# Making a projected weight in four double bursts instead of eight, with its input tiles in lent buffers

## The chip, the core and the metric

The kernel runs on one core of a Trainium2 chip. The core has five engines with an instruction order of their own: TensorE (PE: matmuls; PEld: its weight loads), VectorE (DVE), ScalarE (ACT), GpSimd (POOL) and SyncE (SP, which here only issues transfers). They meet through semaphores: an instruction whose input or whose output place isn't free holds up everything behind it in its engine's order. Matmuls add up in PSUM, which has eight banks (b0 to b7); everything else lies in SBUF. The metric is the device time of one execution in microseconds, median of several runs.

## The reference, cut to what matters

Two branches over the same x (2048 tokens, 640 wide), mixed by a gate:

```python
a = einsum("bsd,ed->bse", x, dft_hid_re); b = einsum("bsd,ed->bse", x, dft_hid_im)
y = einsum("ts,bse->bte", dft_seq_re, a) - einsum("ts,bse->bte", dft_seq_im, b)      # branch A

q = einsum("nd,dhc->nhc", xf, w_q)                     # 32 heads, 256 wide
s1 = einsum("nhd,ed->nhe", q[..., :dk], k1); s2 = einsum("nhd,ed->nhe", q[..., dk:], k2)
# top 2 of each, top 2 of their 4 sums, softmax -> g, expert numbers top_e       # branch B
act = gelu(einsum("nd,nhkd->nhk", xf, u[top_e]))
out = einsum("nhk,nhk,nhkd->nd", g, act, v[top_e])

gate = sigmoid((x * gate_w).sum(-1)); result = gate * y + (1 - gate) * out
```

All values are float32. The kernel never forms q: it multiplies w_q by the keys k1 and k2 first, which gives one matrix W' of 640 x 1024 (64 half-heads by 16 keys), and then scores x against W'.

## The kernel before, in words

Each float32 matmul is made of three passes in a reduced format: an operand is split into a rounded half h (ScalarE, line 138) and a remainder l (VectorE or POOL, line 139), and `mm3` (lines 143 to 145) adds h*h, h*l and l*h into a bank.

The first half of the kernel walks over *pieces* (`seq_piece`, line 229). A piece is 128 rows of a sequence matrix by 512 columns: `pieces = [(w, c, s) ...]`, s running fastest over the 16 row tiles, c over 4 column blocks, w over the real and the imaginary matrix. Piece n multiplies x tile s = n % 16 by it into banks 0 to 4, 15 matmuls of 512 columns. Pieces 0 to 15 are the first column block, 16 to 31 the second; behind pieces 15 and 31 ScalarE empties the five banks (line 252), and piece 16 or 32 then begins them anew. While TensorE is at piece n, the program issues the load of piece n + 5 (five buffers, `wf`) and the split of piece n + 3 (a ring of four, `WS`).

Everything else is hung between the pieces by `at(n, f, ...)`: the function f is emitted behind piece n (`follow(n)`), and calls for one n are emitted in the order in which they were registered. Instructions of each engine run in the order in which they were emitted; nobody reorders them. In the first `N0` = 30 pieces these are hung in:

- `load_x` (line 284), `split_x` (290), `gate_sum` (315): behind piece n the load of x tile n + 4, the split of tile n + 3 (ScalarE, VectorE), and the gate's sum of tile n + 2 (VectorE, line 318). Raw x lies in three buffers of two tiles each, with the tags xf, xh, xl.
- `load_wq` and `w_part` (388, 393): w_q comes in 32 tiles of 640 KB, four to each of 8 groups G, into five buffers. A *burst* is the four tiles of a group: 16 float32 matmuls of 320 columns (32 records, line 400), into two banks drawn in turn from 5 and 6 (`ps_s`). When a bank is complete, VectorE transposes it into wp[G] (line 406).
- `split_w` (408) splits wp[G] into W', kept in `WH` and `WL`. `make_t` (415), for groups 4 to 7, makes four sums of W's blocks with six VectorE instructions (lines 428 to 433) and splits them (ScalarE and VectorE, four times) into `TW`, which lies where x tiles 0 to 5 were.
- `put_x` and `get_x` (484, 487): x tiles 0 to 10 are stored to DRAM after use and fetched again; `move_x` copies tiles 11 and 12 aside.
- `load_u`, `split_u` (439, 443): the expert table u, five tiles, split into `UH` and `UL`; `load_xT`, `split_xT` (POOL), `sum_xT` (VectorE, lines 472 to 475): the first pair of transposed x tiles.

Behind piece 31 the scoring begins (`score_step`, 583), four steps to a pair of x tiles, each behind a piece of its own. Its first step uses W' of groups 0 to 3 and bank 5, splits the sums of x (ScalarE, then POOL) and copies a bank (line 587); its second step needs that copy and `TW`.

In the kernel before, group G's burst is hung behind piece 6 + 3G, so at 6, 9, 12 ... 27:

```python
    for G in range(NG):
        b = 6 + 3 * G
        for m in range(4 * G, 4 * G + 4):
            at(b, w_part, m)
        at(b, split_w, G)
        if G >= NG // 2:
            at(b + (4, 3, 2, 1)[G - NG // 2], make_t, G)
```

These lines are registered behind those of x, so behind one piece `load_x`, `split_x` and `gate_sum` come first.

Of the kernel before, what the change touches and what calls it, by code (L numbers as in the profile page):

```python
# [8 lines left out]
F32 = mybir.dt.float32  # L9
F32R = mybir.dt.float32r  # L10
# [7 lines left out]
P = 128  # L18
S = 2048
D = 640  # L20
H = 32
E = 16
HH = 2 * H
WARM = 11
NE = E * E
NT = S // P
NP = NT // 2
TC = 512
NC = S // TC
NPC = 2 * NC * NT  # L30
KD = D // P
HALF = D // 2
NG = HH // 8
# [73 lines left out]
def gated_mix_kernel(ctx: ExitStack, tc: tile.TileContext, xT, xn, dreT, dimT, wsre, wsim, wq, kT, uT, vv, gw, out):  # L107
    nc = tc.nc
# [3 lines left out]
    big = ctx.enter_context(tc.tile_pool(name="big", bufs=1))  # L112
# [5 lines left out]
    def rotate(what, n):  # L118
        turn[what] = (turn.get(what, -1) + 1) % n
        return turn[what]  # L120

    def bank(n, shape=(P, TC), dt=F32):
        return psum.tile(list(shape), dt, name=f"b{n}", tag=f"b{n}")

    def ps_s(shape=(P, TC)):
        return bank(5 + rotate("pss", 2), shape)

    def ps_t(shape, dt=F32):
        return bank(7, shape, dt)

# [5 lines left out]
    def split(f, h, l, eng):  # L136

        nc.scalar.activation(h, f, AF.Copy)  # L138
        eng.tensor_sub(l, f, h.bitcast(F32))  # L139

    def mm3(o, wh, wl, ah, al, first, last, more=False):

        nc.tensor.matmul(o, wh, ah, start=first, stop=False, skip_group_check=more)  # L143
        nc.tensor.matmul(o, wh, al, start=False, stop=False, skip_group_check=more)  # L144
        nc.tensor.matmul(o, wl, ah, start=False, stop=last, skip_group_check=more)  # L145
# [9 lines left out]
    def run_bg(us):  # L155
        bg.run(us, share)


    WU = big.tile([P, 2 * KD * (HH * E + NE)], F32R, name="WU", tag="WU")
    NW = KD * HH * E  # L160
    WH, WL = (WU[:, n * NW:(n + 1) * NW].rearrange("p (k c) -> p k c", k=KD) for n in range(2))
    UH, UL = (WU[:, 2 * NW + n * KD * NE:2 * NW + (n + 1) * KD * NE].rearrange("p (k c) -> p k c", k=KD)
              for n in range(2))
    zc = const.tile([P, NT], F32)
    gt, gc = (const.tile([P, 2 * NT], F32, name=t) for t in ("gt", "gc"))

# [2 lines left out]
    N0 = 3 * NG + 6  # L169
# [26 lines left out]
    def at(n, f, *args):  # L196
        then.setdefault(n, []).append(lambda: f(*args))
# [57 lines left out]
    for q in range(2 * NC):  # L255
        n = NT * (q + 1)
# [83 lines left out]
    t = ps_t([P, TC])  # L340
    for n in range(WARM):
        c = slice(0, 2 * P) if n < WARM - 1 else slice(2 * P, TC)
# [41 lines left out]
    wqs, wps, wp = {}, {}, {}  # L384
    WQB = 5
    NWQ = 4 * NG

    def load_wq(m):
        if m < NWQ:
            wqs[m] = p1.tile([P, 4, HALF], F32, name="wq", bufs=WQB)  # L390
            nc.sync.dma_start(wqs[m], wq[m])

    def w_part(m):
        G, r, n = m // 4, m // 2 % 2, m % 2
        if r == 0:
            wps[G, n] = ps_s()
        ps = wps[G, n]
        w = wqs.pop(m)
        for j in range(4):
            nc.tensor.matmul(ps[32 * j:32 * j + 32, :HALF], kp[:, 8 * G // H, r, :], w[:, j], start=(r == 0),  # L400
                             stop=(r == 1))
        if r == 1:
            if n == 0:
                wp[G] = p1.tile([P, KD, P], F32, name="wp", bufs=2)
            t = wp[G].rearrange("p k (j c) -> p j k c", c=32)[:, 2 * n:2 * n + 2]
            nc.vector.transpose(t, wps.pop((G, n))[:, :HALF].rearrange("p (j k c) -> p j k c", j=2, c=32))  # L406
# [27 lines left out]
        for n in range(1, 5):  # L434
            split(t[:, n - 1], *(w[:, :, c] for w in TW[n]), nc.vector)

    uf = {}

    def load_u(k):
        uf[k] = p1.tile([P, NE], F32, name="uf", tag="uf", bufs=2)  # L440
        nc.sync.dma_start(uf[k], uT[k])

    def split_u(k):
        split(uf.pop(k), UH[:, k], UL[:, k], nc.vector)


    xf, xs = {}, {}
# [41 lines left out]
        nc.sync.dma_start(X[s].bitcast(F32), xd[s])  # L489

    for s in range(9):
        at(6 + 2 * s + (3 if s == 8 else 0), put_x, s)
    for s in range(3):
        at(2 * NT - 5 + s, get_x, s, 6 + s)
    for s, tag in ((11, "xh"), (12, "xl")):
        at(s + 5, move_x, s, tag)
    for n in range(NT - 4):
        at(n, load_x, n + 4)
    for n in range(NT - 3):
        at(n, split_x, n + 3)  # L500
    for n in range(NT - 2):
        at(n, gate_sum, n + 2)
    for m in range(WQB):
        at(m, load_wq, m)

    for G in range(NG):
        b = 6 + 3 * G
        for m in range(4 * G, 4 * G + 4):
            at(b, w_part, m)
        at(b, split_w, G)  # L510
        if G >= NG // 2:
            at(b + (4, 3, 2, 1)[G - NG // 2], make_t, G)
        for i, m in enumerate(range(4 * G + WQB, 4 * G + WQB + 4)):
            at(b + (i // 2 if G < 4 else 0), load_wq, m)
    for s in range(9, AWAY):
        at(b - 1, put_x, s)
    n = b + 2
    at(n - 8, load_xT, 0)
    for k in range(KD):
        at(n - 15 + 2 * k, load_u, k)  # L520
        at(n - 13 + 2 * k, split_u, k)
    for a in range(2):
        at(n - 2, split_xT, 0, a)
    at(n - 1, sum_xT, 0)
# [58 lines left out]
    def score_step(p, a):  # L583
# [4 lines left out]
        if a == 0:  # L588
# [3 lines left out]
            if p % 2:  # L592
                u_pairs(p // 2)
# [170 lines left out]
    def put_act(c, n):  # L764

        if n == 0:
            f = p2.tile([P, TC], F32, name="act")
        elif c < NC - 1:
            f = ROWS[1].rearrange("p a b c -> p (a b c)").bitcast(F32)[:, :TC]
        else:  # L770
            f = big.tile([P, TC], F32, name="act", tag="xf")
        nc.scalar.activation(f, AB.pop(("u", n)), AF.Gelu_apprx_tanh)
        AB["act", n] = f
# [5 lines left out]
    def u_pairs(c):  # L779


        xh, xl = xs["xh"], xs["xl"]

        for n in range(2):
            e = slice(n * P, (n + 1) * P)
            AB["u", n] = ps = bank(7 - n)
            for k in range(KD):
                mm3(ps, UH[:, k, e], UL[:, k, e], xh[:, :, :, k, :], xl[:, :, :, k, :], k == 0, k == KD - 1)
                run_bg(0.68)
            if n == 0:  # L790
                put_act(c, 0)

    for p in range(NP):
        n = N0 + 4 * p + min((p + 1) // 2, 3)
# [3 lines left out]
    for n in range(2 * NT + 3, 4 * NT + 3):  # L798
        s = n % NT
# [104 lines left out]
        while masked or unmasked:  # L904
            yield settle(True)

    DD = VH = VL = None
    draw = {}

    def load_dd(m):  # L910

# [4 lines left out]
                nc.sync.dma_start(draw[m][:, a], (dreT, dimT)[w][k])  # L916

    def split_dd(m, a):
        nonlocal DD
        if DD is None:  # L920
            DD = big.tile([P, 2, 2, KD, D], F32R, name="DD", tag="WU")
        w, k = divmod(2 * m + a, KD)
        split(draw[m][:, a], DD[:, w, 0, k], DD[:, w, 1, k], nc.gpsimd)
        if a == 1:
            draw.pop(m)

# [2 lines left out]
    for m in range(KD):  # L929
        for a in range(2):  # L930
            at(N1 + 6 + 5 * m + 2 * a, split_dd, m, a)
        at(N1 + 11 + 5 * m, load_dd, m + 2)
# [11 lines left out]
    TS, T = {}, {}  # L944
# [6 lines left out]
    def t_sum(k, n, a):  # L951

        m = 8 if k == KD else k
        if n < 2:
            return TS[m][:, (2 * n + a) * 2 * P:][:, :2 * P]
        if n == 2:
            return TS[5 + k // 2][:, (2 * (k % 2) + a) * 2 * P:][:, :2 * P]
        return right(0, a, k)[:, 2 * P:4 * P] if n == 3 else TS[m][:, PAIR + a * P:][:, :P]

    def right(w, a, k):  # L960
        return T[("xh", "xl")[a]][:, w] if k == KD else DD[:, w, a, k]

    def make_sums(k):
        if k in (0, KD):
# [104 lines left out]
    for k, (n, m) in enumerate(((-1, 2), (0, 4), (5, 7), (7, 9), (10, 12))):  # L1069
        n, m = NT * (NC + 2) + n, NT * (NC + 2) + m  # L1070
# [89 lines left out]
    def step(m):  # L1160
        b, (u, k) = m // NSTEP, divmod(m % NSTEP, KZ)
        what = UNITS[u]
        if k == 0:
# [8 lines left out]
        split_step(m + AHEAD)  # L1172
        o, w, w5 = {
            "a11": ("X", lambda a: right(0, a, k)[:, 0:2 * P], lambda a: right(0, a, k)[:, 4 * P:]),
            "a12": ("Z", lambda a: right(1, a, k)[:, 0:2 * P], lambda a: right(1, a, k)[:, 4 * P:]),
            "s1": ("Y", lambda a: t_sum(k, 0, a), lambda a: right(0, a, k)[:, 4 * P:]),
            "s2": ("X", lambda a: t_sum(k, 1, a), None),
# [146 lines left out]
```

## Time and profile before

| | |
|---|---|
| median of 3 runs (lowest to highest) | 749.91 us (749.51 to 750.06) |
| the profiled execution | 749.66 us |
| its span, first to last instruction | 747.8 us |
| TensorE busy | 743.5 us, 99% |
| VectorE, ScalarE, POOL busy | 589.9, 364.2, 342.9 us |
| moved by DMA | 171.11 MB, mean 229 GB/s |

The profile is of one execution. Busy is the union of the instructions' durations; TensorE's matmuls overlap in it, so a TensorE that is 99% busy may still lose time between two starts, which is why starts are compared. "L400" is line 400 of the kernel before. In a row of a timeline stand the start, the duration, the engine and line, the operation, the tile written and the tiles read, the count of records, and in brackets the idle time ahead of it with what ended it. In the chain of waits stand start, duration and what held the end up. In the windows stand the stretch and its length, each engine's busy time (with its count of instructions), TensorE's granted clock, the share of the DMA engines and GB/s.

### The profile page before, as it was taken

What the parts mean: (1) busy time and instruction counts of PE and PEld (TensorE: products, weight loads), DVE (VectorE), ACT (ScalarE), POOL (GpSimd) and SP (SyncE); (2) the same over time, 40 slices, a digit from 0 to 9 for tenths busy, and PEclk for the clock granted to TensorE, in tenths of its full rate; (3) what the DMA queues carried; (4) which work ended last, traced back from release to release, by engine and by line L of the source; (5) the groups of instructions that cost most, each with busy time, mean ns of one, the idle gap of its engine ahead of it and who ended that gap; (6) DMA issues with size and microseconds to landing.
All of it is one profiled execution on the core that took longest, in us unless ns stands there. A gap on an engine that the chain in (4) does not pass through costs nothing.

```text
span 747.8 us, 11144 instructions
## 1 busy us (share of the span) xinstructions
PE 743.5 (99%) x3923; PEld 603.7 (81%) x3923; DVE 589.9 (79%) x744; ACT 364.2 (49%) x664; POOL 342.9 (46%) x287
## 2 busy tenths in 40 slices
PE   9999999999999999999999999999999999999998
PEld 7767777888888888888888888888888888888887
DVE  7865378395999899999999888979999974357651
ACT  4335144543544745555463686633545653443351
POOL 5533225440532424145235456643455793487253
PEclk9999999999999999999999999999999999999999
DMA  9999999787566686972498776479865689775301
GB/s 335 397 384 343 379 357 391 203 218 240 138 173 149 188 240 163 230 200 73 116 400 281 159 167 188 140 239 292 287 214 196 225 263 344 216 236 176 112 29 71
DMA packets 84633, 171.11 MB, mean 229 GB/s; under 512 B 16097, under 2 KB 21601, under 8 KB 84321
## 3 DMA queue, kind: packets, MB, share of 16 engines
q1 hardware_dynamic: 70960, 146.13, 57.5%
q0 software_dynamic: 5472, 9.96, 9.0%
q10 hardware_dynamic: 8144, 14.31, 5.1%
q8 instruction: 31, 0.51, 0.3%
q14 instruction: 26, 0.20, 0.1%
HBM read 136.40 MB, written 32.39 MB: 226 GB/s over the span
## 4 chain that ended last, share of the span: by engine, by line
PE 92%; DMA 6%; DVE 1%; ACT 0%; SPq 0%; issue 0%
PE b L143 30%; PE b L144 30%; PE b L145 30%; DMA xr<-in_xn 3%; DMA wq<-in_wq 3%; PE b L400 2%; PE b L877 1%; DVE xr L318 0%; DVE X L139 0%; ACT X L138 0%; DVE wp L406 0%; SPq L322 0%; SPq L288 0%; ACT WU L138 0%; DVE WU L139 0%
## 5 line engine op out<-in xcount | busy, mean ns | idle before, releaser
L143 PE MATMUL b<-WS,X 128*128 128x512 f32 x620 | 243.3, 392 | 0.0
L144 PE MATMUL b<-WS,X 128*128 128x512 f32 x620 | 241.4, 389 | 0.0
L145 PE MATMUL b<-WS,X 128*128 128x512 f32 x620 | 241.3, 389 | 0.0
L139 POOL TENSOR_TENSOR WS<-wf,WS 128x512 fp32r<-128x512 f32 x89 | 132.8, 1497 | 166.7 <-ACT WS L138 157.5
L143 PEld LDWEIGHTS b<-WS,X 128*128 128x128 f32 x620 | 116.4, 188 | 28.3 <-issue 3.1
L145 PEld LDWEIGHTS b<-WS,X 128*128 128x128 f32 x620 | 116.4, 188 | 24.3
L144 PEld LDWEIGHTS b<-WS,X 128*128 128x128 f32 x620 | 116.4, 188 | 23.5
L138 ACT ACTIVATE WS<-wf 128x512 fp32r<-128x512 f32 x89 | 55.2, 625 | 70.8 <-PE b L145 30.3
L865 DVE TENSOR_TENSOR hot<-rows,wtab 128x1024 f16<-128x1024 f16 x64 | 60.6, 973 | 2.6 <-PE b L877 2.6
L139 POOL TENSOR_TENSOR xl<-xf,xh 128x640 fp32r<-128x640 f32 x16 | 27.0, 1691 | 71.6 <-ACT xh L138 71.6
L587 ACT ACTIVATE sc<-b 128x512 f32<-128x512 f32 x32 | 19.8, 620 | 80.8 <-PE b L145 77.0
L191 POOL DMA_DIRECT2D WS<-in_wsre x30 | 26.4, 879 | 62.3 <-ACT WS L189 60.9
L139 POOL TENSOR_TENSOR WS<-ra,WS 128x512 fp32r<-128x512 f32 x33 | 47.1, 1437 | 14.6 <-ACT WS L138 12.6
L138 ACT ACTIVATE WS<-ra 128x512 fp32r<-128x512 f32 x47 | 29.4, 631 | 42.5 <-PE b L145 28.2
L835 ACT ACTIVATE b<-b,mask 128x128 f32<-128x128 f32 x128 | 43.0, 342 | 13.4 <-PE b L877 10.3
L642 DVE TENSOR_TENSOR eq<-sc,mm 128x1024 f16<-128x1024 f32 x32 | 44.4, 1388 | 0.9
L649 DVE TENSOR_REDUCE tied<-eq 128x64 f32<-128x1024 f16 x32 | 39.0, 1219 | 0.9
L640 DVE TENSOR_REDUCE mm<-sc 128x64 f32<-128x1024 f32 x32 | 38.8, 1211 | 0.2
L139 POOL TENSOR_TENSOR WP<-ra,WP 128x512 fp32r<-128x512 f32 x13 | 19.2, 1491 | 31.0 <-ACT WP L138 30.9
L217 DVE SCALAR_TENSOR_TENSOR ST<-ST,grow 128x512 f32<-128x512 f32 x40 | 31.3, 846 | 1.1 <-DMA grow<-gdr 1.1
L143 PE MATMUL b<-WU,xh 128*128 128x512 f32 x80 | 31.1, 389 | 0.0
L144 PE MATMUL b<-WU,xh 128*128 128x512 f32 x80 | 31.1, 389 | 0.0
(216 smaller groups left out, 1449.8 us busy)
## 6 DMA issues: line engine op xcount, KB each, us to landing
X<-xd SPq DMA_DIRECT2D x36, 640.0 KB, 6.6
wq<-in_wq SPq DMA_DIRECT2D x32, 640.0 KB, 8.2
wf<-in_wsim SPq DMA_DIRECT2D x64, 256.0 KB, 4.8
wf<-in_wsre SPq DMA_DIRECT2D x63, 256.0 KB, 6.7
ra<-pd SPq DMA_DIRECT2D x40, 256.0 KB, 3.2
pd<-ST ACTq DMA_DIRECT2D x35, 256.0 KB, 5.3
WS<-in_wsre POOLq DMA_DIRECT2D x30, 256.0 KB, 6.3
xd<-X SPq DMA_DIRECT2D x11, 640.0 KB, 9.5
```

The costliest lines, as they stand in the source:

```text
L138: nc.scalar.activation(h, f, AF.Copy)
L139: eng.tensor_sub(l, f, h.bitcast(F32))
L143: nc.tensor.matmul(o, wh, ah, start=first, stop=False, skip_group_check=more)
L144: nc.tensor.matmul(o, wh, al, start=False, stop=False, skip_group_check=more)
L145: nc.tensor.matmul(o, wl, ah, start=False, stop=last, skip_group_check=more)
L191: nc.gpsimd.dma_start(l, (wsre, wsim)[w][c, s], accum_op=OP.add)
L217: nc.vector.scalar_tensor_tensor(f, f, -1.0 if w else 1.0, g, op0=OP.mult, op1=OP.mult)
L640: nc.vector.tensor_reduce(m, sc, op=OP.max, axis=AX.X)
L642: nc.vector.tensor_tensor(eq, sc, m[:, :, None].to_broadcast([P, HH, E]), op=OP.is_equal)
L649: nc.vector.tensor_reduce(tied[:, s, ib, :], eq, op=OP.add, axis=AX.X)
L835: nc.scalar.activation(f[:, :, n], f[:, :, n], AF.Copy, scale=mask4[:, n:n + 1])
L865: nc.vector.tensor_tensor(o, a, b, op=op)
```

## The change

- The eight bursts become four of two groups each, behind pieces 10, 16, 22 and 28. The groups of a burst use the same two banks: bank 5 + n, with n the half of the group.
- Within a group the two tiles that add into one bank now come one after the other (tile numbers are permuted when loaded).
- The w_q tiles are loaded on other pieces: 0 to 8 behind pieces 0 to 8, then two or so ahead of each burst. Beside the five buffers they lie in places idle at the time: the places of x tiles 14, 15 and 6 to 8, raw x buffers, and a new tile `wqu`, where u's split table goes later. u's table therefore leaves `WU`, and one slice of a later table (`DD`) lies in its place.
- u is loaded and split on pieces 22 to 28 instead of 14 to 24; the moves of x tiles 11 and 12 go from pieces 16 and 17 to 23 and 24; the store of x tile 8, three fetches of x and the load of x transposed shift by one to three pieces.
- `make_t` of groups 4 to 7 goes from pieces 22, 24, 26, 28 to 23, 24, 28, 29.

```diff
-    def ps_s(shape=(P, TC)):
-        return bank(5 + rotate("pss", 2), shape)
...
+    WU = big.tile([P, 2 * NW], F32R, name="WU", tag="WU")
+    wqu = big.tile([P, 2, 4, HALF], F32, name="wqu", tag="UU")
...
+    BURST = 8
+    LENT_WQ = {5: "X15", 6: "X14", 15: "xl", 16: "xf", 17: "xh", 23: "xl", 29: "X6", 30: "X7", 31: "X8"}
+    LENT_U = {7: 1, 8: 0, 14: 1, 18: 0}
...
-        if m < NWQ:
+        if m in LENT_U:
+            wqs[m] = wqu[:, LENT_U[m]]
+        elif m in LENT_WQ:
+            wqs[m] = big.tile([P, 4, HALF], F32, name="wq", tag=LENT_WQ[m])
+        else:
             wqs[m] = p1.tile([P, 4, HALF], F32, name="wq", bufs=WQB)
-            nc.sync.dma_start(wqs[m], wq[m])
+        nc.sync.dma_start(wqs[m], wq[m // 4 * 4 + m % 2 * 2 + m // 2 % 2])
...
-        G, r, n = m // 4, m // 2 % 2, m % 2
+        G, n, r = m // 4, m // 2 % 2, m % 2
         if r == 0:
-            wps[G, n] = ps_s()
+            wps[G, n] = bank(5 + n)
...
-        at(6 + 2 * s + (3 if s == 8 else 0), put_x, s)
-    for s in range(3):
-        at(2 * NT - 5 + s, get_x, s, 6 + s)
+        at(6 + 2 * s, put_x, s)
     for s, tag in ((11, "xh"), (12, "xl")):
-        at(s + 5, move_x, s, tag)
+        at(s + 12, move_x, s, tag)
...
+    n = N0 - 1
+    for B in range(NWQ // BURST):
+        b = 10 + 6 * B
+        for m in range(BURST * B, BURST * (B + 1)):
             at(b, w_part, m)
+        for a in range(2):
+            G = 2 * B + a
+            at(b + (a if b < n - 1 else 0), split_w, G)
+            if G >= NG // 2:
+                at(min(b + 1, n - 1) + a, make_t, G)
+    for b, m in enumerate((0, 1, 2, 3, 4, 5, 6, 7, 8)):
+        at(b, load_wq, m)
+    for m, b in enumerate((10, 10, 11, 11, 12, 12, 13, 14, 16, 16, 16, 17, 18, 19, 20, 20, 22, 22, 22, 22, 23, 24, 25), 9):
+        at(b, load_wq, m)
     for s in range(9, AWAY):
+        at(n - 3, put_x, s)
+    for s, b in enumerate((28, 28, 29)):
+        at(b, get_x, s, 6 + s)
+    at(n - 7, load_xT, 0)
     for k in range(KD):
-        at(n - 15 + 2 * k, load_u, k)
-        at(n - 13 + 2 * k, split_u, k)
+        at(n - 7 + k, load_u, k)
+        at(n - 5 + k, split_u, k)
```

More of the change, by code (lines that the diff above doesn't have):

```diff
@@ L156, in run_bg @@
         bg.run(us, share)
-    WU = big.tile([P, 2 * KD * (HH * E + NE)], F32R, name="WU", tag="WU")
     NW = KD * HH * E
+    WU = big.tile([P, 2 * NW], F32R, name="WU", tag="WU")
+    wqu = big.tile([P, 2, 4, HALF], F32, name="wqu", tag="UU")
     WH, WL = (WU[:, n * NW:(n + 1) * NW].rearrange("p (k c) -> p k c", k=KD) for n in range(2))
-    UH, UL = (WU[:, 2 * NW + n * KD * NE:2 * NW + (n + 1) * KD * NE].rearrange("p (k c) -> p k c", k=KD)
-              for n in range(2))
     zc = const.tile([P, NT], F32)
@@ L435, in make_t @@
             split(t[:, n - 1], *(w[:, :, c] for w in TW[n]), nc.vector)
-    uf = {}
+    uf, UHL = {}, []
     def load_u(k):
@@ L443, in split_u @@
     def split_u(k):
-        split(uf.pop(k), UH[:, k], UL[:, k], nc.vector)
+        if not UHL:
+            t = big.tile([P, 2, KD, NE], F32R, name="UU", tag="UU")
+            UHL.extend(t[:, n] for n in range(2))
+        split(uf.pop(k), *(t[:, k] for t in UHL), nc.vector)
     xf, xs = {}, {}
@@ L502, in gated_mix_kernel @@
         at(n, gate_sum, n + 2)
[L503 to L508, printed above, removed]
-            at(b, w_part, m)
[L510 to L514, printed above, removed]
+    n = N0 - 1
+    for B in range(NWQ // BURST):
+        b = 10 + 6 * B
+        for m in range(BURST * B, BURST * (B + 1)):
+            at(b, w_part, m)
+        for a in range(2):
[7 more added lines that the diff above has]
+        at(b, load_wq, m)
     for s in range(9, AWAY):
-        at(b - 1, put_x, s)
-    n = b + 2
-    at(n - 8, load_xT, 0)
+        at(n - 3, put_x, s)
+    for s, b in enumerate((28, 28, 29)):
+        at(b, get_x, s, 6 + s)
+    at(n - 7, load_xT, 0)
     for k in range(KD):
-        at(n - 15 + 2 * k, load_u, k)
-        at(n - 13 + 2 * k, split_u, k)
+        at(n - 7 + k, load_u, k)
+        at(n - 5 + k, split_u, k)
     for a in range(2):
@@ L787, in u_pairs @@
             for k in range(KD):
-                mm3(ps, UH[:, k, e], UL[:, k, e], xh[:, :, :, k, :], xl[:, :, :, k, :], k == 0, k == KD - 1)
+                mm3(ps, UHL[0][:, k, e], UHL[1][:, k, e], xh[:, :, :, k, :], xl[:, :, :, k, :], k == 0, k == KD - 1)
                 run_bg(0.68)
@@ L905, in experts @@
             yield settle(True)
-    DD = VH = VL = None
-    draw = {}
+    DD, draw = [], {}
     def load_dd(m):
@@ L918, in split_dd @@
     def split_dd(m, a):
-        nonlocal DD
-        if DD is None:
-            DD = big.tile([P, 2, 2, KD, D], F32R, name="DD", tag="WU")
+        if not DD:
+            t = big.tile([P, 2, 2, KD - 1, D], F32R, name="DD", tag="WU")
+            DD.extend(t[:, :, :, k] for k in range(KD - 1))
+            DD.append(big.tile([P, 2, 2, D], F32R, name="DD", tag="UU"))
         w, k = divmod(2 * m + a, KD)
-        split(draw[m][:, a], DD[:, w, 0, k], DD[:, w, 1, k], nc.gpsimd)
+        split(draw[m][:, a], DD[k][:, w, 0], DD[k][:, w, 1], nc.gpsimd)
         if a == 1:
@@ L960, in right @@
     def right(w, a, k):
-        return T[("xh", "xl")[a]][:, w] if k == KD else DD[:, w, a, k]
+        return T[("xh", "xl")[a]][:, w] if k == KD else DD[k][:, w, a]
     def make_sums(k):
```

## The prediction

> **What bounds the kernel now.** I read the page first, then TensorE's timeline, the chain of waits, the windows, and last the other engines around the two places that the change touches. From the page:
>
> ```profile
> span 747.8 us, 11144 instructions
> PE 743.5 (99%) x3923; PEld 603.7 (81%) x3923; DVE 589.9 (79%) x744; ACT 364.2 (49%) x664; POOL 342.9 (46%) x287
> ```
>
> TensorE is the bound, and almost nothing is left between its instructions. So a microsecond in which it waits is a microsecond lost, and whatever shortens its own stream is gained. TensorE's timeline of the stretch that the change rewrites:
>
> ```profile
> 17.95 0.39 PE L143 MATMUL b<-WS,X 128*128 128x512 f32 x1
> ...
> 27.92 0.39 PE L145 MATMUL b<-WS,X 128*128 128x512 f32 x1
> 28.24 2.36 PE L400 MATMUL b<-wq,kp 128*32 128x320 f32 x32
> 30.53 0.50 PE L143 MATMUL b<-WS,X 128*128 128x512 f32 x1
> 30.87 0.40 PE L144 MATMUL b<-WS,X 128*128 128x512 f32 x1
> ...
> 53.67 1.82 PE L400 MATMUL b<-wq,kp 128*32 128x320 f32 x24
> 55.76 0.75 PE L400 MATMUL b<-wq,kp 128*32 128x320 f32 x8 [0.27 <-DMA wq<-in_wq]
> ```
>
> The first row is the first matmul of piece 4; pieces 4 to 6 are 45 matmuls and end where the first burst begins, so a piece is (28.24 - 17.95 - 0.09)/3 = 3.40 us, or 0.227 us per matmul. Starts, not durations, are to be read: durations overlap. From 27.92 to 30.87 lie 2.95 us; two matmul slots off (0.45) leave 2.50 us as the whole price of a one-group burst. Eight records of a burst take 2.36 - 1.82 = 0.54 us, so 32 take 2.16; the other 0.34 us is the price of entering and leaving a burst. The third burst was cut by a late w_q tile: it ended at 55.76 + 0.75 = 56.51 and not at 53.67 + 2.36 = 56.03, a loss of 0.48 us.
>
> TensorE is full, but in the first 65 us the transfers are full too. The windows (last two columns: share of the DMA engines, GB/s) and the chain of waits:
>
> ```profile
> 5.00:25.00 20.00, 20.00 (x92) 16.59 (x91) 17.29 (x23) 8.61 (x14) 13.60 (x11) 1.00 1.03 397
> 25.00:45.00 20.00, 20.00 (x132) 14.12 (x131) 14.72 (x20) 5.87 (x10) 8.20 (x23) 1.00 1.02 386
> ```
>
> ```profile
> 20.92 9.12 DMA xr<-in_xn
> ...
> 30.07 0.74 ACT X L138
> ...
> 30.84 0.83 DVE X L139
> 31.67 0.73 DVE xr L318
> ...
> 32.41 0.84 DVE wp L406 x2
> ...
> 34.70 10.56 DMA xr<-in_xn
> ```
>
> The chain shows an x tile landing at 30.04 (x9), ScalarE rounding it, VectorE taking the remainder and the gate's sum, and only then VectorE transposing the burst's result, though TensorE had finished that burst at 30.5. The transposes stand behind the x tile in VectorE's order. Today this costs nothing: the next burst, which needs the banks, comes three pieces later.
>
> **The change, part by part.**
>
> *Fewer entries.* Eight bursts become four: 4 x 0.34 = 1.35 us less on TensorE (at least 0.8, if only the 0.09 before and 0.11 behind a burst are saved). The matmuls are the same; their order inside a group changes which of two banks comes when, and I price that at nothing, since successive matmuls of a piece already accumulate into one bank at 0.227. The 0.48 us of the third burst should go too: the new loads for a burst are issued pieces ahead.
>
> *A new wait in the first burst.* Both groups of a burst use banks 5 and 6. Group 1's first matmul must wait until VectorE has transposed group 0's first bank, with the whole of TensorE's order behind it. In VectorE's order of piece 10 stand, ahead of that transpose, the remainder of x13 and the gate's sum of x12. When does x13 land? It is issued at piece 9, in both kernels behind the same transfers: from x9 on, four w_q tiles (5 to 8), four pieces, two stores of x and x10 to x13.
>
> ```profile
> 36.93 0.33 SPq L288 DMA_DIRECT2D xr<-in_xn  x1
> ```
>
> ```profile
> xr<-in_xn SPq DMA_DIRECT2D x1, 320.0 KB, 9.8
> ```
>
> ```profile
> wq<-in_wq SPq DMA_DIRECT2D x32, 640.0 KB, 8.2
> ...
> wf<-in_wsre SPq DMA_DIRECT2D x63, 256.0 KB, 6.7
> ...
> xd<-X SPq DMA_DIRECT2D x11, 640.0 KB, 9.5
> ```
>
> Measured, x13 lands at 36.93 + 9.8 = 46.7. By bytes: 4 x 640 + 4 x 256 + 2 x 640 + 4 x 320 = 6144 KB, 6.29 MB, at 386 to 400 GB/s 15.7 to 16.3 us behind 30.04: 45.8 to 46.3. It cannot come earlier because SP waits less: the DMA share is already over 1. I take 46.2. Then 0.75 (ScalarE) + 0.83 + 0.82 (VectorE, rows of the chain) + 0.42 (half of the two transposes) = 49.0. TensorE, with no burst at pieces 6 and 9, ends piece 10 at 17.95 + 7 x 3.40 = 41.75 and group 0 at 41.75 + 0.09 + 2.16 = 44.0. It stands **5.0 us**. Bounds: 4.4 with the landing at 45.8; 6.8 with 46.7 and VectorE's instructions at their slow price, which they have while POOL works:
>
> ```profile
> 51.84 1.91 DVE L318 CUSTOM_DVE_ANT_0 xr<-xr,gwb 128x640 f32<-128x640 f32 x1
> ```
>
> The bursts behind 16 and 22 have no x tile ahead of their transposes; a bank is free about 0.6 us after its matmuls and asked for 1.1 us after them. No stall there.
>
> *The last burst moves from piece 27 to 28 and holds two groups.* Let E be the first matmul behind it. Now and here:
>
> ```profile
> 117.71 2.36 PE L400 MATMUL b<-wq,kp 128*32 128x320 f32 x32
> 120.00 0.50 PE L143 MATMUL b<-WS,X 128*128 128x512 f32 x1
> ...
> 135.09 0.39 PE L143 MATMUL b<-WS,X 128*128 128x512 f32 x1
> ```
>
> ```profile
> 119.60 1.06 DVE L406 STREAM_TRANSPOSE wp<-b 128x320 f32<-128x320 f32 x2 [1.43 <-PE b L400]
> 121.25 0.56 DVE L139 TENSOR_TENSOR WU<-wp,WU 128x384 fp32r<-128x384 f32 x1 [0.59 <-ACT WU L138]
> 121.72 0.42 DVE L428 TENSOR_TENSOR tt<-wp,WU 128x256 f32<-128x256 f32 x1
> ...
> 128.84 0.42 DVE L139 TENSOR_TENSOR WU<-tt,WU 128x256 fp32r<-128x256 f32 x1
> 129.18 1.52 DVE L472 TENSOR_TENSOR xf<-xf 128x256 f32<-128x256 f32 x1
> ```
>
> ```profile
> 131.25 0.63 ACT L189 ACTIVATE WS<-WS 128x512 fp32r<-128x512 f32 x1
> 131.78 2.75 ACT L252 ACTIVATE ST<-b 128x512 f32<-128x512 f32 x5
> ...
> 135.66 0.58 ACT L587 ACTIVATE b<-b 128x512 f32<-128x512 f32 x1
> ```
>
> Piece 32 needs the banks that ScalarE empties behind piece 31, and asks for the first at 135.09, E + 15.1 today. Behind piece 28 one piece less lies between: E + 11.7. ScalarE reaches that emptying only through its order: halves of both groups' W', of group 6's sums, of u's last tile, piece 32, halves of group 7's sums, pieces 33 and 34. The sums of a group (ten VectorE instructions) took 128.84 + 0.42 - 121.72 = 7.5 us beside POOL, and 3.85 without it, by these rows (nine in 3.47):
>
> ```profile
> 98.37 0.41 DVE L429 TENSOR_TENSOR tt<-wp 128x256 f32<-128x256 f32 x1
> ...
> 101.42 0.42 DVE L139 TENSOR_TENSOR WU<-tt,WU 128x256 fp32r<-128x256 f32 x1
> ```
>
> ```profile
> 121.92 3.36 POOL L139 TENSOR_TENSOR xl<-xf,xh 128x640 fp32r<-128x640 f32 x2 [2.61 <-ACT xh L138]
> ```
>
> In the new order that POOL work (x transposed, piece 27) is done before the burst, and POOL waits for ScalarE, so I take the fast price. From E: W' of both groups ready 1.8 (121.81 - 120.00 today), group 6's sums 5.65, u 6.0, the sums of x 8.8 (four instructions: 1.7 all fast, 3.9 with two at the 1.52 of L472, taken 2.8 with one), group 7's last half on ScalarE 8.8 + 2.4 + 0.5 = 11.7, pieces 33 and 34 three times 0.6, 13.5, the first emptying 14.1. Piece 32 starts 2.4 late. ScalarE goes on: four more emptyings 2.2, four halves of x's sums 1.4, the copy of the bank (L587) 0.55, at 18.3; TensorE is through piece 32 at 14.1 + 3.4 = 17.5 and waits 0.8 more. Together **3.2 us**; bounds 0, if ScalarE gets through its list 3 us faster than summed, and 7, if one group's sums keep their slow price.
>
> *At nothing.* The w_q tiles in lent places: the raw x buffers and u's table are idle then; the latest, in X8, can be issued when piece 24 is through, 13.6 us before the burst behind 28, against 10.6 us, the longest landing quoted; without that cover the burst would wait up to the difference. u's tiles come two pieces before they are split, 6.8 us, and have landed in up to 10.6; SP runs about three pieces ahead of TensorE, which covers it; if not, VectorE is late for the last burst by about 3 us, and that goes into the upper bound. The two moved copies of x on ScalarE fall at pieces 23 and 24 with no one waiting. The table's new place is read as before.
>
> *The sum.* Against the profiled execution's own 749.66: 749.66 - 1.35 - 0.48 + 5.0 + 3.2 = 756.0. That execution is 0.25 under the median, so **756.3**.
>
> **The rivals.** *The first stall alone* (VectorE and ScalarE keep up after piece 28): 753.1. For it: today's list ends well ahead of 135.09; against it: it gets twice the work and one piece less.
>
> *No stall; the bursts only merge.* 749.91 - 1.35 - 0.48 = 748.1, faster. The mechanism is the landing of x13: from 49.0 back to 44.0, it would have to land by 41.2, that is 5 us before the bytes allow it. Against it is the DMA share of 1.02; for it, only that the lent places let SP issue w_q tiles 5 to 8 earlier. The second stall would have to vanish too.
>
> *Both stalls, and a slow clock behind the first.* At the start TensorE ran 256 columns in 0.23 us, half the pace of later:
>
> ```profile
> 0.77 2.51 PE L343 MATMUL b<-const-bfloat16-1.0 128*128 128x256 bf16 x11 [0.77 <-PEq L1316]
> ```
>
> If a wait of 5 us puts it back into that state for as long as this row lasts, 2.51 us pass at half pace and 1.25 are lost: 757.6. The trace has no wait of that length to show it. [...]
>
> *More than summed* (slow sums in the last burst, or a late u tile): 749.91 - 1.83 + 5.0 + 7 = 760.1, and 763.1 with 6.8 in the first burst and the clock.
>
> **How the numbers follow.** Both stalls 0.47 (its own range 754 to 759), with the slow clock 0.12, first stall alone 0.16, more than summed 0.09, no stall 0.16. The range leaves out the last and the top of the one before: 752 to 762.5. Some 0.2%, 1.5 us, is what a measurement here tells from no change. No stall lies at the edge of it: 0.10 faster, 0.06 same; with 0.02 from a smaller first stall, same is 0.08, slower 0.82.
>
> **What would show it.** Right: a gap on TensorE inside the first burst, between the 32nd and the 33rd record, ended by VectorE's L406; a gap before piece 32 ended by ScalarE's L252; four bursts of 64 records at about 4.6 us where nothing waits. Wrong: a first burst of 64 records without a gap (then x13 was there, and the queue of transfers is not what I read), piece 32 on time, or a burst waiting for a w_q tile.

## The result and the profile after

The changed kernel takes 755.43 us (median), the kernel before 749.91: a ratio of 1.0077, 95% interval 1.0051 to 1.0102. It is slower, by some 5 us. Its undisturbed runs fall in three places: 754.31, 754.50 and 754.75 at a granted TensorE clock of 1.00, 756.11 at 0.998, and 759.20 at 0.993; a sixth run, at 825.99 us with a clock of 0.851, was disturbed and counts in the median but not in the ratio, and so does one of 930.95 us (0.753) in the first experiment. The profiled execution is the one of 754.75 us. In the changed kernel the lines are renumbered: L405 is the burst's matmul (was L400), L411 the transpose (was L406), L140 to L142 are `mm3`, L135 and L136 the two halves of a split, L314 is the gate's sum, L248 the emptying of the banks (was L252).

The head of the page after:

```profile
span 753.0 us, 11145 instructions
PE 743.4 (99%) x3923; PEld 604.8 (80%) x3923; DVE 577.6 (77%) x744; ACT 366.1 (49%) x664; POOL 341.7 (45%) x287
```

The span grew by 5.2 us, TensorE's busy time not at all. So TensorE waits longer, and the page alone doesn't say where. TensorE's timeline of the kernel after does:

```profile
18.76 0.39 PE L140 MATMUL b<-WS,X 128*128 128x512 f32 x1
...
42.65 2.36 PE L405 MATMUL b<-wq,kp 128*32 128x320 f32 x32
48.05 1.82 PE L405 MATMUL b<-wq,kp 128*32 128x320 f32 x24 [3.03 <-DVE wp L411]
...
120.78 0.39 PE L142 MATMUL b<-WS,X 128*128 128x512 f32 x1
121.09 4.51 PE L405 MATMUL b<-wq,kp 128*32 128x320 f32 x64
125.54 0.50 PE L140 MATMUL b<-WS,X 128*128 128x512 f32 x1
125.88 0.40 PE L141 MATMUL b<-WS,X 128*128 128x512 f32 x1
...
137.00 0.39 PE L142 MATMUL b<-WU,xl 128*128 128x512 f32 x1
139.85 0.50 PE L140 MATMUL b<-WS,X 128*128 128x512 f32 x1 [2.46 <-ACT ST L248]
```

Inside the first burst, group 0's 32 records are issued by 42.65 + 2.16 = 44.81, and the next record starts at 48.05: 3.24 us lost, ended by VectorE's transpose. The last burst, whose banks come free in time, runs through: from the matmul ahead of it to the second one behind it lie 5.10 us, 4.65 without two matmul slots, against 2 x 2.50 for two single bursts, so 0.35 us is saved. Piece 32 starts 2.85 us behind the matmul ahead of it and not 0.23: 2.62 us lost, ended by ScalarE's emptying. The chain of waits of the kernel after tells what lies behind both:

```profile
36.77 8.43 DMA xr<-in_xn
45.23 0.75 ACT X L135
45.99 0.83 DVE X L136
46.82 0.73 DVE xr L314
47.56 0.44 DVE wp L411
48.05 2.36 PE b L405 x32
...
136.74 0.44 DVE tt L438
137.52 0.61 ACT WS L135
138.13 0.53 ACT WS L184
139.22 0.59 ACT ST L248
139.85 0.50 PE b L140
```

First x13's landing, its two halves, the gate's sum of x12, and only then the transpose for which TensorE waits; later VectorE's last sum of group 7, then ScalarE's pieces 33 and 34, and only then the emptying of piece 31's banks.

The landing ends the first wait, but it is only just the last thing waited for. VectorE's timeline has the gate's sum of x11 right ahead, and VectorE then stands idle for 0.40 us until x13's first half is there:

```profile
43.69 1.90 DVE L314 CUSTOM_DVE_ANT_0 xr<-xr,gwb 128x640 f32<-128x640 f32 x1
...
45.99 0.83 DVE L136 TENSOR_TENSOR X<-xr,X 128x640 fp32r<-128x640 f32 x1 [0.40 <-ACT X L135]
```

So an earlier x13 alone would have taken at most 0.40 us off the wait; the rest is what else stands ahead of the transpose in VectorE's order.

The terms add up: 749.66 (profiled execution before) - 4 x 0.35 - 0.48 + 0.81 (piece 4 begins at 18.76, not at 17.95) + 3.24 + 2.62 + 0.34 (three gaps of 0.11 to 0.12 behind the start of piece 32: two restarts and the copied bank) = 754.79; the profiled execution after took 754.75.

### The profile page after: what moved, and what is told of

The parts are those of the page before. It is cut to its first block, busy times and chain, and to the rows that moved or that the text cites. A ratio compares the mean times of both kernels' runs of the same rounds, so it can differ in the third digit from the quotient of the medians.

```text
span 753.0 us, 11145 instructions
## 1 busy us (share of the span) xinstructions
PE 743.4 (99%) x3923; PEld 604.8 (80%) x3923; DVE 577.6 (77%) x744; ACT 366.1 (49%) x664; POOL 341.7 (45%) x287
## 4 chain that ended last, share of the span: by engine, by line
PE 91%; DMA 4%; DVE 3%; issue 1%; ACT 0%; SPq 0%; ACTq 0%
PE b L140 30%; PE b L142 29%; PE b L141 29%; PE b L405 2%; DMA xr<-in_xn 2%; DMA wq<-in_wq 1%; PE b L888 1%; DMA wf<-in_wsre 1%; DVE xr L314 1%; DVE X L136 0%; DVE WU L136 0%; ACT X L135 0%; DVE xf L481 0%; DVE wp L411 0%; DVE tw L136 0%
## 5 line engine op out<-in xcount | busy, mean ns | idle before, releaser
L140 PE MATMUL b<-WS,X 128*128 128x512 f32 x620 | 243.0, 392 | 2.5 <-ACT ST L248 2.5
L142 PE MATMUL b<-WS,X 128*128 128x512 f32 x620 | 241.3, 389 | 0.0
L136 POOL TENSOR_TENSOR WS<-wf,WS 128x512 fp32r<-128x512 f32 x89 | 133.2, 1499 | 173.0 <-ACT WS L135 171.8
L140 PEld LDWEIGHTS b<-WS,X 128*128 128x128 f32 x620 | 116.4, 188 | 29.0 <-ACT ST L248 2.9
L142 PEld LDWEIGHTS b<-WS,X 128*128 128x128 f32 x620 | 116.4, 188 | 24.3
L135 ACT ACTIVATE WS<-wf 128x512 fp32r<-128x512 f32 x89 | 55.7, 626 | 84.1 <-PE b L142 55.6
L876 DVE TENSOR_TENSOR hot<-rows,wtab 128x1024 f16<-128x1024 f16 x64 | 57.9, 931 | 4.4 <-PE b L888 4.4
L136 POOL TENSOR_TENSOR xl<-xf,xh 128x640 fp32r<-128x640 f32 x16 | 26.8, 1675 | 73.5 <-ACT xh L135 67.1
L136 POOL TENSOR_TENSOR WS<-ra,WS 128x512 fp32r<-128x512 f32 x33 | 46.7, 1424 | 14.4 <-ACT WS L135 12.4
L135 ACT ACTIVATE WS<-ra 128x512 fp32r<-128x512 f32 x47 | 29.4, 631 | 42.4 <-PE b L142 28.2
L136 POOL TENSOR_TENSOR WP<-ra,WP 128x512 fp32r<-128x512 f32 x13 | 19.0, 1471 | 31.2 <-ACT WP L135 31.2
L876 DVE TENSOR_TENSOR hot<-hot,rows 128x1024 f16<-128x1024 f16 x32 | 31.5, 985 | 0.0
L140 PE MATMUL b<-WU,xh 128*128 128x512 f32 x80 | 31.2, 391 | 0.0
```

The source lines that it names most:

```text
L876: nc.vector.tensor_tensor(o, a, b, op=op)
```

## The experiments

The theory: two waits, independent of each other, make up the whole loss; the first is as long as x13's landing is late, the second as long as the list ahead of ScalarE's emptying. The rivals: the waits only show a loss that has its cause elsewhere (the transfers, a slower clock), so that taking one away gives nothing back; or the slow clock behind a wait is a large part of it. Each experiment is an edit of the changed kernel, compared with the kernel before on the same chip (749.67 to 749.82 us).

**The first burst cut in two: its second group behind piece 11.**

```diff
-            at(b, w_part, m)
+            at(b + (1 if B == 0 and m >= 4 else 0), w_part, m)
```

> The second group of the first burst is hung behind piece 11 instead of piece 10; nothing else changes. Theory (group 1 waits in the middle of the burst for transposes that stand behind x13 in VectorE's order): group 1 starts 3.4 us later, after the transposes, so the gap of 3.2 us inside the first burst is gone and one more burst entry (0.34) is paid; the profiled kind of run goes from 754.75 to about 751.9. Rival (the gap comes from the pairing of groups in two banks as such, the transposes being too slow for TensorE): the gap moves with group 1 and stays near 3 us, 754 to 755.

Measured 752.81 us, ratio 1.0036 (1.0024 to 1.0048). TensorE's timeline:

```profile
42.03 2.36 PE L405 MATMUL b<-wq,kp 128*32 128x320 f32 x32
...
48.19 1.82 PE L405 MATMUL b<-wq,kp 128*32 128x320 f32 x24 [0.17 <-DVE wp L411]
...
136.88 0.50 PE L140 MATMUL b<-WS,X 128*128 128x512 f32 x1 [2.75 <-ACT ST L248]
```

One piece of other work between the two groups covers the landing, all but 0.17 us. Of the 3.2 us, 2.5 are gained: executions at a mean clock of 1.00 took 751.55 to 752.47 us, where the changed kernel's took 754.31 to 754.75. The entry into a fifth burst costs some 0.35, and the second wait stays, 0.3 longer. So the first wait is a loss of its own.

**x13 loaded one piece later**, the same wait made longer:

```diff
-        at(n, load_x, n + 4)
+        at(n + (1 if n == 9 else 0), load_x, n + 4)
```

> The load of x13 is issued behind piece 10 instead of 9, behind one piece and one store of x more: 256 + 640 KB, at 400 GB/s 2.3 us later; nothing else changes. Theory (x13's landing sets the length of the first stall one to one): the gap in the first burst grows from 3.2 to about 5.5 us, 757 us. [...] Rival (the gap is set by something else): no change, 754.8.

Measured 760.69 us, ratio 1.0137 (1.0122 to 1.0151). TensorE's timeline, then its windows (columns as in the windows before: busy times of PE, PEld, VectorE, ScalarE and POOL, then the granted clock):

```profile
42.13 2.36 PE L405 MATMUL b<-wq,kp 128*32 128x320 f32 x32
49.24 3.43 PE L405 MATMUL b<-wq,kp 128*32 128x320 f32 x24 [4.75 <-DVE wp L411]
```

```profile
45.80:49.21 3.41, 0.00 (x0) 0.00 (x0) 2.02 (x5) 0.74 (x1) 0.00 (x0) 1.00 1.02 410
49.21:52.63 3.42, 3.39 (x28) 1.37 (x32) 0.89 (x2) 1.26 (x2) 1.27 (x1) 0.50 1.05 411
```

The wait grows by 1.7 us, from 3.03 to 4.75 idle, where 2.3 was expected. It follows the landing: x13's second half began at 47.19 us instead of 45.99, 1.20 later, and group 1 at 49.24 instead of 48.05, 1.19 later; the rest of the growth is TensorE, which reached the burst 0.52 earlier. And here is the slow clock: 24 records take 3.43 us where they took 1.82, with a granted clock of 0.50 for 3.42 us. Half of that is 1.7 us lost, an estimate. One such stretch lowers the mean clock of an execution by 0.5 x 3.41 / 753 = 0.002, so by this estimate a mean of 0.998 is one stretch and 0.993 three. This trace is of the execution at 757.67 us, with 0.998; the other three, 760.62 to 761.09, show 0.993, and where their two further stretches lie no trace shows. The changed kernel's own runs fit: 756.11 is 754.5 + 1.7, and 759.20 is about 754.5 + 3 x 1.7.

**The first burst ahead of x13 in every engine's order**, so that VectorE's transposes no longer stand behind it:

```diff
+    for m in range(BURST):
+        at(10, w_part, m)
...
-        for m in range(BURST * B, BURST * (B + 1)):
+        for m in range(BURST * B, BURST * (B + 1) if B else 0):
```

> The first burst stays whole and behind piece 10, but is emitted ahead of the split of x13 and the sum of x12, so that VectorE's transposes come ahead of them; loads and places are the same. Theory (the order on VectorE makes the stall): the transposes now wait only for the gate's sum of x11, which ended at 45.5 in the changed kernel; group 1 starts at about 46.1 instead of 48.07, the gap shrinks from 3.2 to 1.2 us, 752.7. Rival (the landing of x13 or the transfers hold TensorE by another way, for instance through ScalarE or through the w_q tiles): the gap stays near 3 us, 754.8.

Measured 752.63 us, ratio 1.0043 (1.0030 to 1.0055). TensorE's timeline of the burst, then VectorE's around it:

```profile
42.68 2.44 PE L405 MATMUL b<-wq,kp 128*32 128x320 f32 x32
45.42 1.88 PE L405 MATMUL b<-wq,kp 128*32 128x320 f32 x24 [0.30 <-DVE wp L411]
```

```profile
43.03 1.90 DVE L314 CUSTOM_DVE_ANT_0 xr<-xr,gwb 128x640 f32<-128x640 f32 x1
...
44.86 0.90 DVE L411 STREAM_TRANSPOSE wp<-b 128x320 f32<-128x320 f32 x2
```

The transpose now waits for nothing but the gate's sum ahead of it, and about 0.6 us of the 3.2 are left (45.42 - 42.68 - 2.16). It was the order, not the two banks, that made most of the wait: with the same banks and x13 loaded as before, most of it is gone. The time fell by less, 1.9 us between executions at a mean clock of 1.00 (middle ones 754.50 and 752.63). This trace doesn't tell why: its execution shows a mean clock of 0.949, with which the first burst's 32 and 24 records took 2.44 and 1.88 us instead of 2.36 and 1.82, while the matmuls of the piece behind it kept their 0.227 us from start to start (24 of them in 5.46 us, 48.14 to 53.60).

**The last burst behind piece 27 instead of 28**, to give ScalarE one piece more.

```diff
-        b = 10 + 6 * B
+        b = (10, 16, 22, 27)[B]
```

> The last burst is hung behind piece 27 instead of 28; the first burst stays whole. Theory (ScalarE reaches the emptying of the banks behind piece 31 too late, because the halves of both groups' sums stand ahead of it): one more piece of 3.4 us lies between, more than the 2.6 us gap, so the gap ahead of piece 32 goes; about 751.9. Rival (the time was lost on the w_q tiles or the scoring's own input, not on ScalarE's order): no gain, 754 to 755, or a wait for the last w_q tile inside the burst.

Measured 755.64 us, ratio 1.0075 (1.0063 to 1.0087): not the 2.6 us expected. Four of the five executions show a mean clock of 0.998; the one at 1.00, the profiled one, took 753.93, 0.4 to 0.8 less than the changed kernel's at that clock. The second wait stayed, 2.30 us of idle time. What had changed is in the timeline of all engines:

```profile
121.42 0.74 ACT L135 ACTIVATE xh<-xf 128x640 fp32r<-128x640 f32 x1 [0.58 <-DMA xd<-X]
...
122.24 3.47 POOL L136 TENSOR_TENSOR xl<-xf,xh 128x640 fp32r<-128x640 f32 x2 [4.50 <-ACT xh L135]
...
122.49 1.79 DVE L136 TENSOR_TENSOR UU<-uf,UU 128x256 fp32r<-128x256 f32 x1
...
124.20 1.78 DVE L433 TENSOR_TENSOR tt<-wp,WU 128x256 f32<-128x256 f32 x1
...
125.67 1.47 POOL L136 TENSOR_TENSOR WS<-wf,WS 128x512 fp32r<-128x512 f32 x1
...
125.91 1.51 DVE L434 TENSOR_TENSOR tt<-wp 128x256 f32<-128x256 f32 x1
```

POOL's split of the transposed x, and a piece's split behind it, now ran beside VectorE's work, and three instructions that take 0.42 us alone took 1.5 to 1.8. The emptying began 16.92 us behind the burst (138.39 - 121.47), and 13.68 in the changed kernel (139.22 - 125.54): of the 3.4 us won, 3.2 were spent again. The split is late because ScalarE's half of it waits for the store of an x tile. The same edit **together with the cut of the first burst**:

> Both edits together. Theory: the two stalls are independent and both go: 754.75 - 2.9 - 2.9, about 749.0, and against the kernel before some 1.0 (three entries saved) and 0.5 (its late w_q tile) less, 748.4 to 749.0. Rival (the stalls cover for each other, a stall avoided at the first burst comes back as another): 751 to 752.

Measured 752.63 us, ratio 1.0036 (1.0024 to 1.0048): the first wait gone, the second there (2.31 us idle), for the same reason: the same three instructions took 1.5 to 1.8 us.

**The stores of x9 and x10 five pieces earlier**, alone:

```diff
-        at(n - 3, put_x, s)
+        at(n - 8, put_x, s)
```

> The changed kernel with only the stores of x9 and x10 moved from piece 26 to 21; bursts where they were. Theory: POOL's half of x transposed ends before the last burst, which takes 0.9 us from the first remainder behind the burst (1.44 to 0.52) and nothing else, as the sums there already run at the fast price; the gap ahead of piece 32 shrinks from 2.6 to about 1.7, 753.8. Rival (stores don't matter here, the burst's place alone does): no change, 754.8. The first stall stays at about 3 us either way.

Measured 754.88 us, ratio 1.0070 (1.0057 to 1.0084). The second wait fell as expected, from 2.46 to 1.54 us idle, since VectorE's first instruction behind the burst no longer ran beside POOL (0.52 us instead of 1.44). Yet the time hardly moved: in all five runs the mean clock was 0.998, so a slow stretch, 1.7 us by the estimate above, ate what was won. The windows of this kernel and of the changed one around the first wait:

```profile
43.48:46.89 3.41, 1.36 (x22) 0.39 (x12) 3.00 (x6) 0.74 (x1) 0.69 (x1) 1.00 1.02 411
46.89:50.31 3.42, 3.00 (x24) 1.19 (x28) 1.28 (x3) 1.25 (x2) 1.27 (x1) 0.50 1.02 393
```

```profile
43.55:46.96 3.41, 1.47 (x24) 0.46 (x16) 3.01 (x5) 0.74 (x1) 1.36 (x1) 1.00 1.03 396
46.96:50.38 3.42, 2.33 (x33) 0.98 (x33) 1.95 (x5) 1.70 (x3) 0.62 (x1) 1.00 1.01 392
```

Behind a first wait of 2.48 us idle the granted clock was 0.50 here, behind one of 3.03 us in the profiled execution of the changed kernel it stayed at 1.00.

**Both: the cut, the last burst behind 27, and the stores early.**

> As e3 (first burst cut in two, last burst behind piece 27), and the stores of x9 and x10 are hung behind piece 21 instead of 26, where the transfers have room. Theory, mended after e2 and e3: the stall ahead of piece 32 is the length of VectorE's and ScalarE's list behind the last burst; in e2 and e3 that list got longer by what the burst came earlier, because x transposed could not be split before the stores of x9 and x10 had landed, and its POOL half ran beside VectorE's sums (1.5 to 1.8 us for 0.42). With the stores early that half is through before the burst, the sums keep their fast price, ScalarE is at the banks some 4 us earlier and no gap is left: the 2.7 us of e3 go, 749.0, or 748.3 to 749.0 with no run on a halved clock. Rival (the list is late for another reason, the sums of x or ScalarE's own order): the gap stays at 2 us or more, 751.5 to 752.6.

Measured 751.53 us, ratio 1.0025 (1.0016 to 1.0034): again the second wait stayed, 1.89 us idle. The stores were in time, but ScalarE's half of the split still stood behind W' in its order, as the timeline of all engines shows:

```profile
117.31 0.52 ACT L135 ACTIVATE WU<-wp 128x384 fp32r<-128x384 f32 x1 [3.12 <-DVE wp L411]
...
118.04 0.72 ACT L135 ACTIVATE xh<-xf 128x640 fp32r<-128x640 f32 x1
...
118.84 3.41 POOL L136 TENSOR_TENSOR xl<-xf,xh 128x640 fp32r<-128x640 f32 x2 [3.30 <-ACT xh L135]
...
120.75 1.78 DVE L136 TENSOR_TENSOR UU<-uf,UU 128x256 fp32r<-128x256 f32 x1
```

**The same, and the split of the transposed x one piece earlier**, ahead of the burst:

```diff
-        at(n - 2, split_xT, 0, a)
+        at(n - 3, split_xT, 0, a)
```

> As e5, and x transposed is split behind piece 26 instead of 27, so that in ScalarE's order its two halves stand ahead of the last burst's W' half (in e5 they stood behind it, and POOL's part still ran beside VectorE's sums). Theory, mended again: what makes the gap ahead of piece 32 is the length of the list VectorE and ScalarE have behind the last burst, and what makes that list slow is POOL working beside it. Now POOL's part ends near the burst's end; the first four instructions behind it (1.48, 1.78, 1.51, 0.41 in e5) run at 0.52, 0.42, 0.42, 0.41, 3.4 us are won on the list against a gap of 2.05: no gap ahead of piece 32, no run on a halved clock, 751.4 less 2.3, about 749.1; against the kernel before three entries and one late tile, 1.5 us, so 748.3 to 749.1. Rival (the gap follows the list's end wherever it is, because the list itself waits for something with the pieces, like the banks or the sequence matrix): 1 to 2 us of gap stay, 750.5 to 751.4.

Measured 748.73 us, ratio 0.9987 (0.9978 to 0.9996) over 11 runs, 748.24 to 749.22: faster than both kernels, by 0.13%, which is near the limit of what can be told. The timeline of this kernel, all engines in order of time:

```profile
48.26 1.82 PE L405 MATMUL b<-wq,kp 128*32 128x320 f32 x24
...
113.18 1.35 ACT L135 ACTIVATE xh<-xf 128x640 fp32r<-128x640 f32 x2
...
113.98 3.07 POOL L136 TENSOR_TENSOR xl<-xf,xh 128x640 fp32r<-128x640 f32 x2 [1.03 <-ACT xh L135]
...
120.54 0.41 DVE L136 TENSOR_TENSOR UU<-uf,UU 128x256 fp32r<-128x256 f32 x1
...
132.61 2.53 ACT L248 ACTIVATE ST<-b 128x512 f32<-128x512 f32 x5
...
133.81 0.39 PE L142 MATMUL b<-WU,xl 128*128 128x512 f32 x1
134.04 0.39 PE L140 MATMUL b<-WS,X 128*128 128x512 f32 x1
```

POOL is through at 117.05, VectorE's instructions are back at 0.41, ScalarE empties at 132.61, and piece 32 follows at the usual 0.23 us. No wait is left at either place. The sum for this kernel is 749.66 - 3 x 0.35 (five bursts) - 0.48 + 0.50 (its piece 4 begins at 18.45) = 748.6; the profiled execution took 748.73. So the two waits were the whole loss beside the slow clock. What is left of the gain is 0.9 us as measured (749.67 - 748.73), and 1.5 by the sum without the later start: 1.05 from three entries and 0.48 from the w_q tile that is no longer late.

**The first burst whole and ahead of x13, one half of it in a third bank**, with the rest of the last kernel:

```diff
-            wps[G, n] = bank(5 + n)
+            wps[G, n] = bank(7 if (G, n) == (1, 0) else 5 + n)
```

> The last burst as in e8; the first burst whole behind piece 10 and ahead of x13's split as in e7, and its third bank is bank 7, idle at that time, instead of bank 5, so that TensorE needs the first transpose 1.1 us later. Theory: e7's remaining stall of 0.47 us is the wait for that one transpose and goes, and the entry of 0.34 that the cut first burst paid is saved: 0.3 under e8, 748.0 to 748.8. Rival (a wait for the transposes returns at the fourth bank): level with e8 or 0.3 above it.

Measured 748.60 us, ratio 0.9984 (0.9975 to 0.9993). This kernel's result is not the reference's, for a reason that no run here shows, so its time is read for the wait only: 56 records take 4.12 us by starts (42.37 to 46.49) where 3.78 is usual, some 0.3 us more; at which bank no row here shows. So a loss as long as the rival's came back: with one burst fewer the kernel is no faster than the kernel of five bursts by anything that can be told (748.24 to 749.75 against 748.24 to 749.22).

## Why the prediction was right, point by point

**Where the loss lies.** Right at both places, with the releasers named: VectorE's transpose inside the first burst, ScalarE's emptying ahead of piece 32. The other bursts waited for nothing, no w_q tile was late in the profiled execution, and four merged bursts gave 4 x 0.35 where 4 x 0.34 was taken. The case "both stalls" came true; 755.43 lies 0.9 under the 756.3 given and within that case's own range. Part of that nearness is luck: the 756.3 assumes the full clock, at which the executions took 754.31 to 754.75, and those with slow stretches lift the median.

**The first stall was mis-sized: 5.0 taken, 3.24 measured,** below even the lower bound of 4.4 (4.6 by that bound's own landing of 45.8). Two things differ. x13's split began at 45.23, and its landing was taken at 46.2: the term "6.29 MB at 386 to 400 GB/s" was too slow a rate. In the kernel after, x9's split began at 29.92, so the same bytes took some 15.3 us, 411 GB/s. That put the transpose's end at 48.05 where 49.0 was taken, 0.95 early. And TensorE came 0.81 late: piece 4 began at 18.76. The second part changes nothing in the total, since the stall ends when x13 lets it, wherever TensorE stands; it only moves 0.81 us from the stall to the start. So the one error of weight in the sum is the landing. (The sum takes 0.82 for the gate's sum where its chain has 0.73, which is worth 0.1.) What the path leaves out is VectorE's own work, which lasted until 0.40 us before x13's first half was ready.

**The second stall: 3.2 taken, 2.96 measured.** The emptying was forecast to be through with its first bank at E + 14.1, with E the first matmul behind the burst; it came at 139.85 - 125.54 = 14.3. 2.62 us were lost and not 2.4, but the copied bank and the restarts cost 0.34 and not 0.8. One premise failed: POOL's split of the transposed x was not done before the burst but at 125.90 (122.82 + 3.08), and VectorE's first remainder behind the burst took 1.44 us instead of 0.52. The sum still held, since that remainder began 0.57 us behind E and not 1.25 as in the row it was taken from. The choice of the fast price for group 6's sums held (0.41 to 0.43 us each in the profile); that the slow one was near shows in three of the kernels with the last burst behind piece 27, where three instructions in a row met it (1.5 to 1.8 us each).

**The slow clock.** It was given as a case of its own at 0.12, tied to the first stall and priced at 1.25 us: by the author's estimate a wait of 5 us would bring back the pace of the start for the 2.51 us of one row. No run has a wait of 5 us, and none shows a slow stretch of that length behind one. What the traces show in its place is a granted clock of 0.50 for 3.41 to 3.42 us at a time, 1.7 us by half of it: behind the first wait in two variants (x13 later, the stores early alone), behind the second in three (the cut, both, both with the stores early). Between executions of one kernel at a mean clock of 0.998 and at 1.00 the middle times lie 1.0 us (both with the stores early) to 1.8 us (the last burst earlier) apart, 1.6 in the changed kernel. There a mean below 1.00 came at 756.11 us (0.998) and 759.20 (0.993) and not at 754.31 to 754.75: the same kernel has it in one execution and not in another.

**"No stall".** The rival of 748.1 was refused because x13 would have to land 5 us earlier. The experiments show that it didn't need to: the cut, or the order, takes most of the wait away with x13 loaded as it is, and with the second wait gone too the kernel lands at 748.7, 0.6 above that rival. The refusal was right for this change, not for the idea behind it.

**The start.** Not foreseen. Piece 4 began at 17.95 in the one trace of before, and between 18.14 and 18.79 in the ten of the changed kernel and its variants, which are nearly alike up to there. Whether the w_q loads that now begin at piece 0 add a part to this spread is not settled by any run.

## What to carry to other kernels

When two pieces of work that share output buffers are put back to back, look at who frees the buffer between them and at what stands ahead of it in that engine's order: here the freeing took 0.44 us but stood behind an x tile that landed at 45.20 us and behind two more instructions, TensorE lost 3.24 us, and one piece of other work in between, or the other order, took most of that wait away. When work is put nearer to a deadline, sum the whole list of every engine between them, and check which of its instructions will now run beside another engine that slows them (0.42 us became 1.5 to 1.8 here): three attempts to gain a piece's time lost most of it to that, until the work on the other engine went ahead too.

## What the runs showed of the hardware that was not expected

The granted clock can be halved at a wait of TensorE, and the length of the wait alone doesn't tell when. In five traces one stretch of 3.41 to 3.42 us has a granted clock of 0.50 and the stretches before and behind it 1.00; it begins between 0.42 us before the end of the wait (stores early) and 0.87 us behind it (both with stores early). The waits were 4.75 us of idle time (x13 later), 2.75 (the cut), 2.48 (stores early), 2.31 (both) and 1.89 (both with stores early). Behind waits of 3.03 and 2.46 us (the changed kernel), 2.30 (last burst earlier) and 1.54 (stores early, the second wait) the clock stayed at 1.00. The busy time of TensorE doesn't tell it either: the 3.41 us just ahead of the half-clock stretch held 0.00 us of it (x13 later), 0.83 (the cut), 1.36 (stores early), 1.10 (both) and 1.52 (both with stores early), but 3.41 us of the changed kernel, 137.00 to 140.41, held 0.95 and the clock stayed. What decides it was not shown. The windows of the variant with both and the stores early have the highest busy time that a half-clock stretch followed:

```profile
133.38:136.79 3.41, 1.52 (x7) 0.93 (x6) 2.08 (x6) 3.38 (x8) 2.46 (x2) 1.00 0.00 0
136.79:140.21 3.42, 3.42 (x10) 2.64 (x9) 2.75 (x4) 3.39 (x10) 2.00 (x3) 0.50 0.61 77
```

A wait of 2 to 3 us thus has two prices in these runs, its own length and some 1.7 us more or not; that makes the kernel's times fall in steps (754.31 to 754.75, 756.11, 759.20), and a shorter wait can cost more than a longer one (2.48 us with a slow stretch against 3.03 without). And VectorE's float32 sums of two 128x256 operands took 0.41 us alone (both with the stores early and the split ahead) and up to 1.78 beside POOL's split (last burst earlier), four times as long.
